# One-token gated attention and MLP on one core: the sixth value tile loaded in one transfer, the seventh in three, and the output projection's Pool-queue rows moved as 32 KB pieces instead of 16 KB

## The chip, the cores and the metric

The kernel runs on one core of a Trainium2 chip, in one launch. The metric is the device time in microseconds (us). The kernel before took 192.69 us, the median of three runs (192.54 to 192.71).

## The reference

One token of 512 numbers goes through two branches, which a gate mixes. Everything is bfloat16.

```python
g = sigmoid((x * gate_w).sum(-1))
q = (x @ wq) as 32 heads of 128
scores = q . k_cache * 128**-0.5        # 32 heads, 4096 cached keys each
p = softmax(scores)
a = (p @ v_cache, heads joined) @ wo    # wo is 4096 x 512
h = relu(x @ w1 + b1) ** 2              # 1376 wide
b = h @ w2 + b2
out = g * a + (1 - g) * b
```

The two caches are 32 MB each, `wq` and `wo` 4 MB each, `w1` and `w2` 1.4 MB each. Every byte is read once.

## The kernel before

**Tiles.** Four heads make a group, so there are NT = 8 groups and 8 key tiles and 8 value tiles. A tile is 128 partitions of 32 KB, 4 MB: each head has 32 partitions, each with B = 128 consecutive keys of 128 numbers. All tiles, and late in the kernel the tile "m" of small weights, go through five buffers of the tensor `ring`, in the order of the list `LOADS`: k0, k1, k2, v0, k3, v1, k4, v2, k5, v3, k6, v4, k7, v5, v6, m, v7. The SP queue issues them in that order. Before each, the function `free` (L304 to L310) waits until the buffer's last user is done: for a key tile VectorE's products and TensorE's transposes, for a value tile TensorE's products with it.

**Compute.** A group is worked in U = 4 units. Of a key tile's 128 columns VectorE multiplies 80 with the query (`ttr`, L734; 96 in the last tile), and TensorE transposes the other 48, which ScalarE copies out and TensorE multiplies with the query (`transposes`, `evac`, `scores`). Maximum, exponentials and the products with the value tile (`pv`) follow. TensorE's program is a loop over i from 0 to NU + 1 with NU = 32 units; the table `PV` says which `pv` units are run at which i. For the last groups the table is written by hand: units 20 and 21 (the first half of v5, the sixth value tile) at i = 30, units 22 to 27 (the rest of v5 and all of v6) at i = 32, after the last scores. The four units of v7 come later, behind the output projection's first part.

**Values in parts.** `PARTS` names the value tiles that are loaded in several transfers, and where they are cut, in columns. Each part has a semaphore of its own, and `pv` waits for a part at the unit that starts on its cut. Before, v5 comes in two parts of 64 columns, v6 in four of 32, v7 in parts of 40, 40, 36 and 12. A row of 64 columns is 16 KB in one partition, one of 32 columns 8 KB. A tile that is not in `PARTS` comes in one transfer of 32 KB rows, and `landed` waits for its buffer's semaphore.

**wo.** The projection's weights for 28 of the 32 heads are 112 rows of 32 KB, and each row goes to one partition of the tensor `W`, where `wq` was before. They follow when the queries are made (`started`). The list `FIRST` has eight transfers of three rows each, which SP issues between v0 and k3 (L325). The list `RUNS` has ten transfers, which the Pool queue issues (L376): rows 24, 24, 4, 8, 4, 8, 4, 8, 2 and 2, 88 in all. A run has a number e and a width k. `place` puts its rows on partitions from 32 + 4e + r on, or from 4e + r on (64 + 4e + r from e = 8), four partitions further for each step of e. `turns` reckons a position `at` from 0 to 15 that a run of width k moves on by k; where the next run's e is not the present position, a dummy transfer of d rows is issued ahead of it to make up the difference (L373). Seven such dummies are issued, of 4, 4, 4, 4, 4, 3 and 2 rows; each row is two pieces of 8 bytes. The runs' e are 4, 4, 4, 8, 4, 8, 4, 8, 3 and 7, their widths k 12, 12, 4, 8, 4, 8, 4, 8, 2 and 2. `max_dma_last_dim=16384` cuts each 32 KB row of a run into two pieces; the transfers of `FIRST` have no such cap. Which row landed in which partition is undone at the end by the 0/1 matrix `selA` (`spread_a`).

**End.** After VectorE's last products: the sums and outputs of groups 5 and 6, `spread_a`, 22 of the 32 column blocks of `wo` on TensorE (`out_a`) and 10 on VectorE (`rows_v`), the MLP, the four units of v7, then `out_b` with the last four heads' rows of `wo` (the last transfers but one), `mlp_out`, and the store.

Of the kernel before, what the change touches and what calls it, by code (L numbers as in the profile page):

```python
# [5 lines left out]
def bass_gated_mix__gqa_block_cached__dense_activation_squared_relu__decode_kernel(  # L6
# [34 lines left out]
    NT = NH // R  # L41
    B = 4096 // P

    U = 4
    NU = NT * U
# [7 lines left out]
    PV = {i: [i - LAG] for i in range(LAG, LAG + (NT - 3) * U)}  # L53
# [2 lines left out]
    PV[27] = [18, 19]  # L56
    for i in (28, 29, 30):
        del PV[i]
    PV[NU - 2] = [NU - 3 * U, NU - 3 * U + 1]
    PV[NU] = list(range(NU - 3 * U + 2, NU - U))  # L60

    PARTS = {NT - 3: [0, 64, B], NT - 2: [0, 32, 64, 96, B], NT - 1: [0, 40, 80, 116, B]}

    GR = [(0, 8), (8, 16), (16, 24), (24, 28), (28, 32)]
    NG = len(GR)
# [32 lines left out]
    def turns():  # L98
        at, out = 0, []
        for _, e, k, _, _ in RUNS:  # L100
            d = (e - at) % 16
            out.append((False, d) if d != 1 else (True, e))
            at = (e + k) % 16
        return out
# [29 lines left out]
    with ctx:  # L134
# [6 lines left out]
        def sem(name):  # L141
            return ctx.enter_context(nc.semaphore(name))
# [3 lines left out]
        def held(kind, j=0):  # L146
            return ring[:, AT[kind, j] % SLOTS, :]
# [93 lines left out]
        s_wp = [sem(f"s_wp{n}") for n in range(len(RUNS))]  # L241
        s_dm = [sem(f"s_dm{n}") for n in range(len(RUNS))]
        s_wr = sem("s_wr")
        s_wk = sem("s_wk")
        s_vl = {(j, n): sem(f"s_vl{j}{n}") for j in PARTS for n in range(len(PARTS[j]) - 1)}
        s_sel = sem("s_sel")
# [65 lines left out]
        def started(eng):  # L312
            eng.wait_ge(s_qps, NT)
            eng.wait_ge(s_g, 4)
            eng.wait_ge(s_b1c, 1)

        @block.sync
        def _(eng):
            for n, (kind, j) in enumerate(LOADS):  # L320
                free(eng, n)
                if n == SLOTS - 1:
                    started(eng)
                    for p, st, k, q in STRIPS[len(RUNS):]:
                        eng.dma_start(W[p:p + st * (k - 1) + 1:st, :], woa_v[q:q + k, :]).then_inc(s_wr, 16)  # L325
                if kind == "v" and j in PARTS:
                    for w in range(len(PARTS[j]) - 1):
                        part = slice(PARTS[j][w] * 128, PARTS[j][w + 1] * 128)
                        eng.dma_start(held("v", j)[:, part], v_v[j][:, part]).then_inc(s_vl[j, w], 16)  # L329
                elif kind in "kv":  # L330
                    eng.dma_start(held(kind, j), (k_v if kind == "k" else v_v)[j])\
                       .then_inc(s_l[n % SLOTS], 16)
                elif kind == "m":
                    eng.dma_start(held("m")[:, 0:W2], w1_v).then_inc(s_w[0], 16)
                    eng.dma_start(held("m")[:, W2:W3], w2_v).then_inc(s_w[1], 16)
            for c in range(len(TS) - 1):
                eng.dma_start(wob_sb[:, TS[c]:TS[c + 1], :], wob_v[:, TS[c]:TS[c + 1], :])\
                   .then_inc(s_wo[c], 16)
            eng.dma_start(w2b, B_w2[F - 128:F, :]).then_inc(s_w[2], 16)
            eng.wait_ge(s_f4, 1)  # L340
            eng.dma_start(out[0, 0, :].rearrange("(j p) -> j p", p=128), fin4).then_inc(s_out, 16)

        @block.gpsimd
        def _(eng):
            eng.memset(ident[:, :], 0.0).then_inc(s_id, 1)
            eng.memset(identf[:, :], 0.0).then_inc(s_id, 1)
            eng.memset(onesf[:, :], 1.0).then_inc(s_cst, 1)
            eng.wait_ge(s_id, 2)
            for m in (ident, identf):  # L350
                eng.affine_select(out=m[:, :], in_=m[:, :], compare_op=ALU.not_equal, fill=1.0,
                                  base=0, pattern=[[-1, 128]], channel_multiplier=1)\
                   .then_inc(s_id, 1)
            eng.memset(RS[:, :], 0.0).then_inc(s_cst, 1)
            eng.memset(E[:, :, :, :], 0.0).then_inc(s_cst, 1)
            eng.memset(selA[:, :, :], 0.0).then_inc(s_sel, 1)
            eng.wait_ge(s_sel, 1)
            for n, (p, st, k, q) in enumerate(STRIPS):
                eng.wait_ge(s_sel, n + 1)
                part = selA[:, :, p:p + st * (k - 1) + 1]  # L360
                eng.affine_select(out=part, in_=part, compare_op=ALU.not_equal, fill=1.0, base=-st * q,
                                  pattern=[[st, 4], [-1, st * (k - 1) + 1]], channel_multiplier=4 * st)\
                   .then_inc(s_sel, 1)

            started(eng)
            sent = 0
            for n, ((back, d), run) in enumerate(zip(turns(), RUNS)):
                if back:
                    eng.inc_swdge_sem([], [], mode="reset_dge_cursor")  # L370
                if d:
                    src = B_w1[0:d, 0:32].rearrange("p (a c) -> p a c", a=2)
                    eng.dma_start(dm[0:d, sent, :, 0:4], src[:, :, 0:4]).then_inc(s_dm[sent], 16)  # L373
                    sent += 1
                p, st, k, q = STRIPS[n]
                eng.dma_start(W[p:p + st * (k - 1) + 1:st, :], woa_v[q:q + k, :],  # L376
                              max_dma_last_dim=16384).then_inc(s_wp[n], 16)
            for n in range(sent):
                eng.wait_ge(s_dm[n], 16)
            eng.wait_ge(s_wr, 16 * len(FIRST))  # L380
            for q in s_wp[:-1]:
                eng.wait_ge(q, 16)
            eng.wait_ge(s_wp[-1], 16)
            eng.memset(tick[:, :], 0.0).then_inc(s_wk, 1)
# [76 lines left out]
        def _(eng):  # L461
# [82 lines left out]
            def pv(u):  # L544
                j, w = u // U, u % U
                lo, hi = w * B // U, (w + 1) * B // U
                if j == NT - 1:
                    lo, hi = PARTS[j][w:w + 2]
                if j in PARTS:
                    if lo in PARTS[j]:  # L550
# [320 lines left out]
```

## Time and profile before

| | before |
|---|---|
| median of three runs | 192.69 us |
| the profiled execution | 192.5 us, of which the span from first to last instruction 191.1 us |
| VectorE, TensorE, ScalarE busy | 83%, 64%, 44% of the span |
| moved by DMA | 78.70 MB, mean 412 GB/s |
| packets | 5298, of them 768 on the Pool queue (q0), 2.89 MB |
| mean granted TensorE clock | 0.674 |

The span is cut into 40 slices in the page's second part; a digit there is the busy share in tenths. SPq and POOLq are the queues that issue transfers; a "landing" is the time from the issue of a transfer to its semaphore. The trace also has a record of every DMA packet, with its queue, size, start and duration, but without the engine that moved it.

### The profile page before, as it was taken

The numbers are of one execution on the slowest core, as the hardware profiler recorded it, in microseconds if no ns is written. First come the engines' busy times: TensorE is split into PE (matmuls) and PEld (weight loads), VectorE is DVE, ScalarE is ACT, GpSimd is POOL, SyncE is SP. The second block draws the span as 40 slices with busy tenths as digits, with TensorE's granted clock in tenths as the row PEclk, the third lists the DMA queues.
The fourth block names the chain that finished last, engine by engine and source line by source line (L and its number), as shares of the span: only waits on it lengthen the run. The fifth ranks groups of instructions, "written<-read, shape, count | busy, mean of one in ns | idle before, by whom it ended". The sixth has DMA issues, their size and how long they took to land.

```text
span 191.1 us, 5609 instructions
## 1 busy us (share of the span) xinstructions
PE 122.1 (64%) x1864; PEld 92.8 (49%) x1866; DVE 158.6 (83%) x1387; ACT 84.3 (44%) x207; POOL 18.4 (10%) x48
## 2 busy tenths in 40 slices
PE   0019764644524694898499986845876488548975
PEld 0014343534413543276256544745876277437964
DVE  0031399999999999999999999998999799998821
ACT  2013975825843654077409542943644293000400
POOL 7630000990000000000000000000000000000000
PEclk9999998555555558699859759955555555555555
DMA  6999999999999999999999999999999999999992
GB/s 219 440 440 439 439 439 430 439 398 451 432 424 405 432 406 432 442 420 439 442 427 422 425 434 425 417 424 432 425 430 435 398 424 406 419 421 426 414 388 72
DMA packets 5298, 78.70 MB, mean 412 GB/s; under 512 B 1099, under 2 KB 1741, under 8 KB 1870
## 3 DMA queue, kind: packets, MB, share of 16 engines
q1 hardware_dynamic: 4488, 75.47, 93.1%
q0 software_dynamic: 768, 2.89, 3.7%
q8 instruction: 14, 0.23, 0.5%
q14 instruction: 14, 0.11, 0.2%
q10 hardware_dynamic: 14, 0.01, 0.0%
HBM read 78.35 MB, written 0.00 MB: 410 GB/s over the span
## 4 chain that ended last, share of the span: by engine, by line
DVE 46%; DMA 38%; SPq 7%; PE 4%; ACT 2%; issue 2%; DVEq 0%; ACTq 0%
DVE ring L734 43%; DMA ring<-in_A_k_cache_dram 25%; DMA ring<-in_A_wo_dram 14%; SPq L329 6%; DVE S L734 2%; PE pX L562 2%; ACT E L434 1%; PE KP L516 1%; PE pO L576 1%; ACT kT L415 0%; DVE gm L748 0%; DVE gx L751 0%; ACT parts L440 0%; PE pQ L637 0%; DVE mp L741 0%
## 5 line engine op out<-in xcount | busy, mean ns | idle before, releaser
L734 DVE CUSTOM_DVE_ANT_0 ring<-ring,qb 128x128 bf16<-128x128 bf16 x656 | 140.6, 281 | 1.4 <-DMA ring<-in_A_k_cache_dram 1.3
L415 ACT ACTIVATE kT<-KP 128x768 bf16<-128x768 bf16 (+1 forms) x64 | 46.6, 779 | 47.1 <-PE pQ L529 19.0
L734 DVE DVE_READ_ACCUMULATOR2_ANT S<- 128x1 f32 x656 | 50.5, 77 | 0.1
L516 PE MATMUL KP<-ident,ring 128*128 128x128 bf16 x368 | 37.9, 275 | 9.5 <-DMA ring<-in_A_k_cache_dram 6.2
L516 PEld LDWEIGHTS KP<-ident,ring 128*128 128x128 bf16 x368 | 30.9, 126 | 14.1 <-DMA ring<-in_A_k_cache_dram 6.5
L562 PE MATMUL pX<-ring,E 128*16 128x512 bf16 x72 | 24.0, 493 | 0.0
L434 ACT ACTIVATE E<-S,nM 32x128 bf16<-32x128 f32 x32 | 18.6, 580 | 1.0
L570 PE MATMUL pO<-E,ring 128*128 128x4 bf16 x352 | 10.8, 166 | 4.9 <-DMA ring<-in_A_v_cache_dram 4.9
L570 PEld LDWEIGHTS pO<-E,ring 128*128 128x128 bf16 x352 | 10.2, 102 | 5.3 <-DMA ring<-in_A_v_cache_dram 5.2
L536 PE MATMUL pM<-identf,mp 128*1 128x128 f32 x8 | 3.0, 370 | 15.1 <-DVE mp L741 15.1
L562 PEld LDWEIGHTS pX<-ring,E 128*16 128x16 bf16 x72 | 6.9, 106 | 11.5 <-issue 7.7
L570 PE MATMUL pX<-E,ring 128*128 128x4 bf16 x384 | 11.3, 166 | 1.6 <-DMA ring<-in_A_v_cache_dram 1.6
L570 PEld LDWEIGHTS pX<-E,ring 128*128 128x128 bf16 x384 | 11.0, 105 | 1.8 <-DMA ring<-in_A_v_cache_dram 1.8
L426 ACT ACTIVATE nM<-pM 128x1 f32<-128x1 f32 x8 | 1.4, 174 | 19.0 <-PE pM L541 19.0
L529 PE MATMUL pQ<-qcol,kT 128*128 128x4 bf16 x176 | 7.7, 168 | 2.3 <-ACT kT L415 2.3
L541 PE MATMUL pM<-onesf,gx 1*128 1x1 f32 x16 | 4.2, 329 | 7.0 <-DVE gx L751 7.0
L529 PEld LDWEIGHTS pQ<-qcol,kT 128*128 128x128 bf16 x176 | 7.1, 105 | 3.1 <-ACT kT L415 3.1
L536 PEld LDWEIGHTS pM<-identf,mp 128*1 128x1 f32 x8 | 0.7, 85 | 16.3 <-DVE mp L741 16.1
L700 DVE CUSTOM_DVE_ANT_0 ring<-ring 1x512 bf16<-1x512 bf16 x1 | 0.7, 680 | 9.4 <-DMA ring<-in_gate_w_dram 9.4
L529 PEld LDWEIGHTS pS<-qcol,kT 128*128 128x128 bf16 x192 | 7.4, 106 | 1.7 <-issue 1.7
L434 ACT ACTIVATION_READ_ACCUMULATOR E<-S,nM 32x1 f32 x32 | 8.1, 253 | 0.0
L529 PE MATMUL pS<-qcol,kT 128*128 128x4 bf16 x192 | 7.7, 168 | 0.0
(88 smaller groups left out, 109.0 us busy)
## 6 DMA issues: line engine op xcount, KB each, us to landing
ring<-in_A_k_cache_dram SPq DMA_DIRECT2D x8, 4096.0 KB, 29.5
ring<-in_A_v_cache_dram SPq DMA_DIRECT2D x5, 4096.0 KB, 29.0
W<-in_A_wq_dram SPq DMA_DIRECT2D x1, 4096.0 KB, 12.4
ring<-in_A_v_cache_dram SPq DMA_DIRECT2D x2, 2048.0 KB, 27.7
ring<-in_A_v_cache_dram SPq DMA_DIRECT2D x4, 1024.0 KB, 27.7
ring<-in_A_v_cache_dram SPq DMA_DIRECT2D x2, 1280.0 KB, 31.9
W<-in_A_wo_dram POOLq DMA_DIRECT2D x2, 768.0 KB, 17.9
ring<-in_B_w_dram SPq DMA_DIRECT2D x1, 1376.0 KB, 25.3
```

The costliest lines, as they stand in the source:

```text
L329: eng.dma_start(held("v", j)[:, part], v_v[j][:, part]).then_inc(s_vl[j, w], 16)
L415: eng.activation(kT[:, n % NC, 0:HB[u // U] * 128], KP[n % 3][:, 0:HB[u // U] * 128], ACT.Copy).then_inc(s_ev, 1)
L426: eng.activation(nM[:, j:j + 1], MB[:, j:j + 1], ACT.Copy).then_inc(s_nm, 1)
L434: eng.activation(E[rows, j % NE, :, r], S[rows, j % NS, :], ACT.Exp, bias=nM[rows, j:j + 1], scale=SCALE, accum_out=RS[rows, R * j + r:R * ...
L516: mm = eng.transpose(KP[n % 3][:, y * 128:(y + 1) * 128], held("k", j)[:, b * 128:(b + 1) * 128], ident[:, :])
L529: mm = eng.matmul(S2[j % 2][:, c:c + R], kT[:, n % NC, y * 128:(y + 1) * 128], qcol[:, R * j:R * j + R], start=True, stop=True)
L536: eng.transpose(MT[0:1, :], mp[:, j:j + 1], identf[:, :]).then_inc(s_mt, 1)
L541: eng.matmul(MB[:, j:j + 1], gx[0:1, j % 2, :], onesf[0:1, 0:1], start=True, stop=True).then_inc(s_mb, 1)
L562: mm = eng.matmul(pX[0:4 * R, :], E[:, j % NE, b:b + 4, :].rearrange("p b r -> p (b r)"), held("v", j)[:, b * 128:(b + 4) * 128], start=(b ...
L570: mm = eng.matmul(O(R * j, R * j + R), held("v", j)[:, b * 128:(b + 1) * 128], E[:, j % NE, b, :], start=(b == n * B // U), stop=(n == 0 a ...
L576: mm = eng.matmul(O(R * j, R * j + R), parts[:, b * 128:(b + 1) * 128], identf[0:4 * R, R * b:R * b + R], start=False, stop=(b == 3), skip ...
L734: ins = eng.tensor_tensor_reduce(kb, kb, qb[:, j, :], 1.0, 0.0, ALU.mult, ALU.add, S[:, j % NS, b:b + 1])
```

## The change

The sixth value tile, v5, is no longer in `PARTS` and comes in one transfer. v6 comes in three parts, of 64, 32 and 32 columns. Units 20 and 21 of `pv` go from i = 30 to i = 32, ahead of units 22 to 27. The ten transfers of `RUNS` have a cap of 32768 bytes for a piece, so that a row of 32 KB is one piece. The dummies and their rows, `place`, `turns` and `FIRST` are as before.

```diff
-    PV[NU - 2] = [NU - 3 * U, NU - 3 * U + 1]
-    PV[NU] = list(range(NU - 3 * U + 2, NU - U))
-
-    PARTS = {NT - 3: [0, 64, B], NT - 2: [0, 32, 64, 96, B], NT - 1: [0, 40, 80, 116, B]}
+    PV[NU] = list(range(NU - 3 * U, NU - U))
+
+    PARTS = {NT - 2: [0, 64, 96, B], NT - 1: [0, 40, 80, 116, B]}
...
                 eng.dma_start(W[p:p + st * (k - 1) + 1:st, :], woa_v[q:q + k, :],
-                              max_dma_last_dim=16384).then_inc(s_wp[n], 16)
+                              max_dma_last_dim=32768).then_inc(s_wp[n], 16)
```

## The prediction

> **What bounds the kernel.** I read the page's slices and queues first, then the chain of waits, then TensorE's timeline at the end, then the records of the DMA packets.
>
> ```profile
> DMA  6999999999999999999999999999999999999992
> GB/s 219 440 440 439 439 439 430 439 398 451 432 424 405 432 406 432 442 420 439 442 427 422 425 434 425 417 424 432 425 430 435 398 424 406 419 421 426 414 388 72
> q1 hardware_dynamic: 4488, 75.47, 93.1%
> q0 software_dynamic: 768, 2.89, 3.7%
> ```
>
> The 16 DMA engines are full from the second slice to the last but one. By the packet records they never run dry between 5 us and 186 us. The Pool queue's share, 3.7%, is wo's ten runs.
>
> ```profile
> 161.90 26.23 DMA ring<-in_A_wo_dram
> 188.27 0.56 PE pQ L637 x16
> 188.84 0.28 PE pQ L628 x4
> 189.37 0.28 PE KP L690
> 189.67 0.21 DVE ring L839
> ```
>
> The chain ends with a transfer that was issued at 161.90 and landed at 188.13: it stood 26 us in a full queue, so a faster or slower issue is nothing to it. Behind it 3.0 us of tail. The time of this execution is 192.5 = 188.1 + 3.0 + 1.4 outside the span; the median is 192.69, 0.2 above.
>
> ```profile
> 160.68 1.87 PE L570 MATMUL pX<-E,ring 128*128 128x4 bf16 x64
> 163.17 1.01 PE L570 MATMUL pO<-E,ring 128*128 128x4 bf16 x32 [0.19 <-DMA ring<-in_A_v_cache_dram]
> 165.64 1.01 PE L570 MATMUL pO<-E,ring 128*128 128x4 bf16 x32 [1.46 <-DMA ring<-in_A_v_cache_dram]
> 168.22 1.01 PE L570 MATMUL pO<-E,ring 128*128 128x4 bf16 x32 [1.57 <-DMA ring<-in_A_v_cache_dram]
> 170.88 1.02 PE L570 MATMUL pO<-E,ring 128*128 128x4 bf16 x32 [1.64 <-DMA ring<-in_A_v_cache_dram]
> 186.27 1.44 PE L570 MATMUL pX<-E,ring 128*128 128x4 bf16 x48 [0.65 <-DMA ring<-in_A_v_cache_dram]
> ```
>
> TensorE waits for data at each quarter of v6 and again, 0.65 us, before the end of v7. VectorE is 83% busy but waits for k6 and k7 too, 0.61 and 0.65 us (131.29 and 150.84 in its timeline). All follow the stream.
>
> A stream ends with its slowest engine, so what each engine has to move counts. The trace names no engine, but the times at which shares of a transfer end show them. After the eight transfers of `FIRST` (24 rows of 32 KB, three a transfer) three shares of k3 end at 71.2 to 71.7, the others mostly at 66.8 to 68.6: three engines carry eight rows each. At k6 fifteen shares end within 127.7 to 129.7, one at 130.8. So the Pool rows went to the others and evened the load; that is what `turns` and the dummies are for. The widths show too: the first 16 KB pieces come in a burst of 12 (40.07 to 40.54), later ones in bursts of 4 (59.5, 61.3) and 8 (64.7).
>
> **Part by part.**
>
> *v5 whole, v6 in three.* Median packet: 1.214 us for 32 KB, 0.614 for 16 KB, 0.312 for 8 KB. Per engine v5 is 8 x 1.214 = 9.71 in place of 16 x 0.614 = 9.82; v6's first half 8 x 0.614 = 4.91 in place of 16 x 0.312 = 4.99. Saved: 0.19 us. SP issues two transfers fewer, about 0.4 us each, hidden by the 26 us of queue.
>
> *`pv` of units 20 and 21 later.* On TensorE they are moved past the scores of unit 30, the transposes of unit 31 and its scores: 64 matmuls, 1.85 us at 156.51. After the change 128 matmuls begin at 160.5 and end at 164.2, the sum at L585 (0.57) at 164.8. v6's first half lands, as its second quarter now, at 165.6; then 64 matmuls, 1.9 us, until 167.5, and the next quarter at 168.2. Cover 0.7 us at both places, so I price this at nothing; without the cover it would add at most what the 0.65 us before 186.27 doesn't take. Nobody else waits: VectorE asks for unit 23 only at 171.33, no buffer and no exponential waits for units 20 to 23, and the scores of units 30 and 31 come up to 1.85 us earlier, to no use.
>
> *wo's rows in one piece.* By packets alone: 2 x 0.611 becomes about 1.214 a row, nothing. Pool issues the same 17 transfers (0.55 to 0.62 us each), and its wait for them, over at 99.76, is needed only at 172.
>
> What isn't shown is where whole rows go. The dummies could do with one piece a row, yet are written with two, as the runs were; `FIRST`, on SP's queue, has whole rows. No row of the trace has whole rows on Pool's queue. Two bounds: (a) the steering holds, no change; (b) each run starts at the first engine, whatever stands before it. In (b) a 24-row run puts two rows on each of engines 0 to 11, the others one row on each of the first 4, 8 or 2. Engines 0 and 1 then get 2 + 2 + 3 x 1 + 3 x 1 + 2 x 1 = 12 rows that they don't have now, beside the 8 of `FIRST`: 20, where now the fullest have 8. I take (b): the two pieces stand in the code exactly at the transfers that are steered and nowhere else, and the cap that made them is what is changed.
>
> [...]
>
> Price of (b): 12 x 1.214 = 14.6 us on engine 0, if a row costs what it costs now. The three `FIRST` engines are not the last at present: two have their share of k7 at about 148.9 and 149.1, the last engine at 150.4, and data stop between 186.1 and 188.4. So 1.5 us are swallowed. About 20 packets in the trace take some 0.6 us more than their kind, 1.25 an engine; those two engines show none, so I add 0.7. Net 14.6 - 1.5 + 0.7 - 0.2 = 13.6, for 206.1.
>
> Upwards: `place` gives each row the partitions of the engine that was to bring it. Under (b) the rows of engine 0 go to partitions that other engines are writing just then. Nothing in the trace prices that; two writers that take turns at worst double the packet, 12 x 1.214 = 14.6 more. The four rows from the wide runs are nearest to now, since all twelve writers are shifted alike and stay out of each other's way: price 0. For the other eight I take the middle between single and double, 8 x 0.61 = 4.9. Sum: 192.5 + 13.6 + 4.9 = 211.0.
>
> [...]
>
> What is late next under (b): k3 to k7 land later by what engine 0 has taken on, and VectorE, which has only 1.3 us of such waits now, waits some 13 to 18 us in all; its tail shifts with k6 and k7, and the end stays with the stream.
>
> **Rivals.**
>
> 1. *The steering holds* (not slower). For it: nothing in `turns`, `place` or the order is changed, and SP's whole rows keep to three engines. Against it: the two-piece dummies. It decides if k6's shares still end within about 3 us. The gains then stand alone, 0.2 of stream (0.06 more where an engine has eight Pool rows): 192.4. Chance 14%.
> 2. *Whole rows spread over 16 engines, but from the cursor.* Only dummies move the cursor then. Adding up the ten runs, engines 0 to 2 get 5 rows beside their 8: 5 x 1.214 = 6.1, less 1.5, plus 0.7, less 0.2, and up to half as much again for shared partitions: about 199. For it: a cursor is what the dummies turn. Against it: a spread over all needs no start. Chance 6%.
> 3. *`pv` late.* If v5's one landing came after 161.2, units 20 to 23 would end behind v6's first half and the delay go on through the sums at L764 to `rows_v`, at most 1 us over the 0.65 of slack: 193.0. Against it: v5's rows are ahead of v6's in the queue, and its second half does not delay 160.68 now. Chance 2%, counted with slower.
>
> Forecast, (b): 78%.
>
> **Numbers.** (b) gives 206.1 with undisturbed rows and 215.9 with eight doubled; 211.0 is its middle. The range goes down to rival 2 and leaves out rival 1 and the far end of doubling: 199 to 216. Runs of this kernel differ by 0.17 us, so about 0.2% (0.39 us) can be told from no change; rival 1's gain of 0.1% mostly can't. Faster 6%, same 8% (both from rival 1), slower 86%.
>
> **What would show it.** Right: 88 packets of 32 KB on q0; shares of k6 that end more than 10 us apart, two last; VectorE waiting for key tiles by over 10 us; a mean of 370 to 385 GB/s (78.70 MB over some 209 us), 9s in the DMA row giving way to 8s and 7s; a landing of the key tiles longer than 29.5 us; the same 3 us tail. Packets on q0 longer than 1.3 us would show shared partitions, 1.21 us would bring 206. Wrong: the row of 9s and 412 GB/s unchanged. Then the end is at 188, and only 0.2 us have gone.

## The result and the profile after

The changed kernel takes 226.26 us, the median of six runs (225.51 to 226.74), beside 192.61 for the kernel before: a ratio of 1.174 (95% interval 1.173 to 1.176), 33.7 us slower. The forecast had the direction and the place, but 211.0 us and at most 216. The profiled execution took 226.74, its span 225.4. Executions over 1.5% above the fastest of their kernel, one of `cursor0` and one of `crossed`, are left out of the times and ratios below.

The page of the changed kernel, slices and queues (one slice is now 5.6 us):

```profile
DMA  7999999998999999899968999999999999999320
GB/s 279 437 402 465 425 406 465 282 353 215 345 279 291 260 262 250 244 361 361 413 269 334 465 385 445 449 390 458 385 451 445 394 420 428 416 409 364 129 107 30
q1 hardware_dynamic: 4200, 75.47, 86.2%
q0 software_dynamic: 576, 2.89, 5.4%
```

Two losses can be seen. From the eighth slice to the nineteenth the engines are as busy as before by the packet records, but move 215 to 361 GB/s, not some 430: the packets themselves are slow. And at the end, 129, 107 and 30 GB/s: four engines are far behind and work alone. The trace's semaphore records show when each share of a transfer ends: of the transfer at the end of the chain below, twelve end between 206.8 and 209.5 us, the other four singly at 220.2, 221.0, 221.7 and 222.4. Between these two losses, in slices 20 to 22, engines stand idle (52 us, summed over the 16 engines).

VectorE's and SP's waits of the changed kernel (engine, line, waited for: us in total, times, longest), and VectorE's timeline where the longest one ends:

```profile
DVE ring L733 <- DMA ring<-in_A_k_cache_dram: 34.0, 5, 30.0
SPq L330 <- PE pO L575: 67.4, 3, 42.3
106.54 0.29 DVE L733 CUSTOM_DVE_ANT_0 ring<-ring,qb 128x128 bf16<-128x128 bf16 x1 [29.99 <-DMA ring<-in_A_k_cache_dram]
```

VectorE waits 34.0 us for key tiles, where it waited 1.3. Thirty of them are one wait, for k3, the tile that follows `FIRST` and shares its time with all of wo's runs. Twelve of its shares end by 85.5 us, the last three at 105.7 to 106.5. While it is missing no buffer comes free, so SP can't issue (42.3 us), and that is the idle of slices 20 to 22. After k3 the kernel runs as it did, late: k6 begins at 165.43 (131.29 before), the span ends 34.3 us later.

The end of the chain of waits has the old form, with a tail of 3 us:

```profile
191.52 30.86 DMA ring<-in_A_wo_dram
222.53 0.56 PE pQ L636 x16
```

The packet records give the sizes. wo's runs are now 88 packets of 32 KB, with a median of 2.18 us each. A row cost two pieces of 0.611 before. Of the tiles' 32 KB packets 348 took over 1.5 us, before 35. Summed over wo's pieces and the 32 KB packets of SP's queue, the time above 1.213 us (0.611 for 16 KB) was 28.4 us before and is 372.2 now: 343.8 more, or 21.5 us for each of 16 engines. I call this the extra packet time.

### The profile page after: what moved, and what is told of

Read it like the earlier page. It is cut to its first block, busy times and chain, and to the rows that moved or that the text cites. A ratio compares the mean times of both kernels' runs of the same rounds, so it can differ in the third digit from the quotient of the medians.

```text
span 225.4 us, 5609 instructions
## 1 busy us (share of the span) xinstructions
PE 122.1 (54%) x1866; PEld 93.1 (41%) x1866; DVE 158.9 (70%) x1387; ACT 84.1 (37%) x207; POOL 18.1 (8%) x48
## 4 chain that ended last, share of the span: by engine, by line
DMA 31%; DVE 26%; another core or an unknown queue 16%; PE 14%; ACT 5%; SPq 4%; issue 3%; ACTq 0%; POOL 0%; POOLq 0%; DVEq 0%
DVE ring L733 24%; DMA ring<-in_A_wo_dram 14%; DMA ring<-in_A_k_cache_dram 13%; PE pX L561 5%; DMA ring<-in_B_b_dram 5%; SPq L328 3%; PE KP L515 3%; ACT E L433 2%; PE pQ L493 2%; ACT kT L414 1%; DVE S L733 1%; ACT qb L405 1%; PE pO L575 1%; PE pX L493 1%
## 5 line engine op out<-in xcount | busy, mean ns | idle before, releaser
L561 PE MATMUL pX<-ring,E 128*16 128x512 bf16 x72 | 23.2, 480 | 2.9 <-DMA ring<-in_A_v_cache_dram 2.9
L799 DVE SCALAR_TENSOR_TENSOR ring<-W,o2f,ring 128x512 f32<-128x512 bf16 x9 | 6.8, 751 | 0.3
## 6 DMA issues: line engine op xcount, KB each, us to landing
ring<-in_A_k_cache_dram SPq DMA_DIRECT2D x8, 4096.0 KB, 30.3
ring<-in_A_v_cache_dram SPq DMA_DIRECT2D x2, 1024.0 KB, 30.3
```

The costliest lines, as they stand in the source:

```text
L561: mm = eng.matmul(pX[0:4 * R, :], E[:, j % NE, b:b + 4, :].rearrange("p b r -> p (b r)"), held("v", j)[:, b * 128:(b + 4) * 128], start=(b ...
L799: eng.scalar_tensor_tensor(out=vsum[:, :], in0=wo_sb[:, TP + t, :], scalar=o2f[:, t:t + 1], in1=vsum[:, :], op0=ALU.mult, op1=ALU.add).the ...
```

## The experiments

Each experiment is the kernel before with the edit shown, unless said otherwise. Where a row has an interval, it is that of the ratio to the kernel before on the same chip.

**1. The two halves of the change.** `parts_only` is the changed kernel with the old cap, `cap_only` the kernel before with the new one.

```diff
 # cap_only; parts_only has all the other lines of the change
-                              max_dma_last_dim=16384).then_inc(s_wp[n], 16)
+                              max_dma_last_dim=32768).then_inc(s_wp[n], 16)
```

> The value tiles' cuts and the order of pv as in the changed kernel, wo's runs in two pieces of 16 KB as before. All theories: the 33.7 us come from the runs, so 192.4 (0.2 under before, from 0.19 us of stream), tiles' packets at 1.21 us throughout. Rival: the tiles' cuts or the late pv have a share in the loss, 193 or more.

> Before with wo's runs in one piece of 32 KB, nothing else changed. All theories: the whole loss, 225.5 to 227. Rival: if the tiles' cuts take part, several us less than 226.

Measured: `parts_only` 192.60 beside 192.72, ratio 0.9993 (0.9984 to 1.0002); `cap_only` 225.1, ratio 1.169 (1.166 to 1.173). The loss is the cap's: 32.4 of the 33.7 us. The tiles' cuts alone gain 0.1 us, which the measurement can't tell from nothing (by the interval, 0.3 gained to nothing). `cap_only` lies 0.4 under what was expected and 1.2 under the changed kernel. Its extra packet time is 326 us, 1.1 less than the changed kernel's for each of 16 engines; whether the tiles' cuts add that under the new cap isn't shown. TensorE's timeline of `parts_only` shows the late `pv`:

```profile
161.11 3.57 PE L569 MATMUL pX<-E,ring 128*128 128x4 bf16 x128 [1.22 <-DMA ring<-in_A_v_cache_dram]
166.01 1.87 PE L569 MATMUL pO<-E,ring 128*128 128x4 bf16 x64 [0.90 <-DMA ring<-in_A_v_cache_dram]
168.48 1.02 PE L569 MATMUL pO<-E,ring 128*128 128x4 bf16 x32 [0.60 <-DMA ring<-in_A_v_cache_dram]
170.97 1.01 PE L569 MATMUL pO<-E,ring 128*128 128x4 bf16 x32 [1.47 <-DMA ring<-in_A_v_cache_dram]
186.37 1.44 PE L569 MATMUL pX<-E,ring 128*128 128x4 bf16 x48 [0.54 <-DMA ring<-in_A_v_cache_dram]
```

TensorE waits for v5's single landing and starts 0.6 us after the 160.5 that was forecast, but still waits 0.90, 0.60 and 1.47 us for v6's three parts and 0.54 before the end: the work stays covered.

**2. Where whole rows go.** `cursor0` keeps two pieces a row and the dummies, and sets the Pool queue's cursor back just ahead of each run.

```diff
                 p, st, k, q = STRIPS[n]
+                eng.inc_swdge_sem([], [], mode="reset_dge_cursor")
                 eng.dma_start(W[p:p + st * (k - 1) + 1:st, :], woa_v[q:q + k, :],
```

> Before with two pieces a row, but the Pool queue's engine cursor set back to the first engine just ahead of every run, so that two-piece runs start where the forecast put whole rows. Theory A (whole rows start at the first engine, and rows written to another engine's partitions are slow on both sides): pieces of 16 KB at 0.95 to 1.2 us, tiles' packets at 1.5 us or more meanwhile, 218 to 228 us. Theory B (whole rows from the Pool queue are slow in themselves, beside the uneven load): pieces stay at 0.61 us and only the uneven load is left, 12 rows on two engines, 204 to 208 us. Theory C (whole rows stay steered and are slow in themselves): also 204 to 208, and the changed kernel would not share its pattern.

Measured: 225.58, ratio 1.169 (1.167 to 1.172), the same ratio as `cap_only`. Pieces of 16 KB now take 0.895 us (median), with 42 of 176 between 0.65 and 0.8, so Theory A's lower bound for a piece was a little high; its time holds. Size and form of the pieces are not the cause; the engine at which a run starts is.

`matched` and `whole_at4` look at it from the other side: whole rows, laid for the engines that get them if a run starts at the first. In `matched` these are four runs of 16 rows. In `whole_at4` they are four runs of 8 rows, each behind a dummy that leaves the cursor at the fifth engine; the other half of those rows comes in two pieces.

```diff
 # matched
-    RUNS = [(INNER, 4, 12, 0, 2), (INNER, 4, 12, 1, 2),
+    RUNS = [(INNER, 0, 16, 0, 1), (INNER, 0, 16, 1, 1), (INNER, 0, 16, 2, 1), (INNER, 0, 16, 3, 1),
             (OUTER, 4, 4, 0, 1), (OUTER, 8, 8, 0, 1), (OUTER, 4, 4, 1, 1), (OUTER, 8, 8, 1, 1),
-            (OUTER, 4, 4, 2, 1), (OUTER, 8, 8, 2, 1),
-            (OUTER, 3, 2, 3, 1), (SEAM, 7, 2, 3, 1)]
-    FIRST = ...
+            (OUTER, 4, 4, 2, 1), (OUTER, 8, 8, 2, 1), (OUTER, 8, 3, 3, 1)]
+    FIRST = [(OUTER, 0, 3, 0, 1), (OUTER, 0, 3, 1, 1), (OUTER, 0, 3, 2, 1)]
...
-                              max_dma_last_dim=16384).then_inc(s_wp[n], 16)
+                              max_dma_last_dim=32768 if k == 16 else 16384).then_inc(s_wp[n], 16)
 # whole_at4, against matched: cursor to 4 ahead of each whole run, to 8 ahead of the others
+    RUNS = [*[(INNER, e, 8, r, 1) for r in range(4) for e in (0, 8)],
...
+            if kind == INNER:
+                out.append((True, 4 if e == 0 else 8))
...
+                              max_dma_last_dim=32768 if run[:2] == (INNER, 0) else 16384).then_inc(s_wp[n], 16)
```

> 64 of the rows as four runs of 16 whole rows of 32 KB on the Pool queue, laid so that the i-th row is on the i-th engine's partitions if a run of whole rows starts at the first engine; the other 48 rows in two pieces, steered, or on SP. Engine 3 gets three rows more than before, the others 7 or 8. Theory A: whole rows at 1.21 us and no tile packet slowed, 192.5 to 196. Theory B (whole rows from the Pool queue are slow in themselves): whole rows at 2.0 us or more, tiles' packets slowed beside them, over 205.

> As matched (same rows on every engine), but the whole rows are four runs of 8, laid for the first eight engines, and ahead of each a dummy leaves the cursor at the fifth engine. If whole rows start at the first engine whatever the cursor is: whole rows at 1.21 us, nothing slowed, 195 to 197 as matched. If they start at the cursor: all 32 of them are on another engine's partitions, whole rows at 2 us, tiles' packets slowed, 203 or more.

Measured: `matched` 195.99, ratio 1.017 (1.015 to 1.019); `whole_at4` 196.43, ratio 1.019 (1.017 to 1.021). In both the whole rows take 1.213 us (median), and the tiles' packets stay at 1.213 to 1.218. So whole rows are not slow in themselves, and with the cursor at the fifth engine they still start at the first. The 3.2 and 3.8 us over before agree with three more rows on engine 3, 3 x 1.213 = 3.6: in both, one share of a late transfer ends 2.6 to 2.9 us behind all others.

**3. The price of other engines' partitions, with even load.** `crossed` was meant for it and wasn't what it was meant to be.

```diff
 # crossed
-    RUNS = [(INNER, 4, 12, 0, 2), (INNER, 4, 12, 1, 2),
+    RUNS = [(INNER, 4, 8, 0, 2), (INNER, 12, 4, 0, 2), (INNER, 4, 8, 1, 2), (INNER, 12, 4, 1, 2),
...
-        for _, e, k, _, _ in RUNS:
+        for kind, e, k, _, _ in RUNS:
+            if kind == INNER:
+                e = 8 if e == 4 else 4
```

> Before with two pieces a row and every engine as many rows as before, but the two 24-row runs cut in 16 and 8 rows whose engines are exchanged, so that 48 of 88 rows are written by an engine four or eight places from the one whose partitions they are. Theory A: the 96 pieces of these rows take over 0.9 us and the other 80 pieces 0.61; four rows an engine by 0.6 to 1.2 us more each, and tiles' packets beside them slower, 195 to 202 us. Theories B and C: all pieces 0.61 us, 192.4 to 193.

Measured: 219.94, ratio 1.142 (1.137 to 1.147), well over what was expected, with slow pieces to the end (in the profiled execution, of 224.3 us, median 0.99 us). The bursts of the kernel before were 12 wide for 24 rows, 8 for 8 and 4 for 4; how wide a run of 16 rows in two pieces goes is in no view. If it is not the eight that `turns` reckons with, the cursor is wrong for every later run, nearly all rows are misplaced, and the load can be uneven too. So it settles nothing by itself. `split_home` and `split_crossed` mend it with runs of 8 and 4 rows:

```diff
 # split_home
-    RUNS = [(INNER, 4, 12, 0, 2), (INNER, 4, 12, 1, 2),
+    RUNS = [*[(INNER, e, k, r, 1) for r in range(4) for e, k in ((4, 8), (12, 4))],
 # split_crossed: split_home, and
+            if kind == INNER:
+                e = 8 if e == 4 else 4
```

> Control for split_crossed: before, with the two 24-row runs cut into eight runs of 8 and 4 rows on the same engines and partitions. Pieces 0.61 us; more turns on the Pool queue, hidden; 192.4 to 193.5.

> The same sixteen runs, but the 8-row runs go to the engines of the 4-row runs and their next ones, and the other way round: every engine has as many rows as in split_home, 48 of 88 rows are written to another engine's partitions. [...] Theory A (another engine's partitions): 96 pieces of 0.75 to 1.3 us, tiles' packets beside them at 1.4 us or more, 200 to 212 us. Theory D (what was lost in the last runs is uneven load alone): pieces 0.61 us, 192.4 to 193.5.

Measured: `split_home` 192.79, ratio 1.0005 (0.9995 to 1.0014); `split_crossed` 206.80, ratio 1.072 (1.067 to 1.077). 48 rows written by an engine that is not their partitions' own cost 14.0 us with the load as even as before. An engine's own partitions are those that `place` pairs with its position in `turns`; no view names them, and what shows the pairing is these two kernels, with the same transfers and the pairing kept (192.79) or broken (206.80). Page of `split_crossed`:

```profile
DMA  7999999999999999999999999999999999999991
GB/s 251 457 425 413 411 451 459 392 336 310 360 339 344 342 315 299 305 355 418 447 413 443 418 426 434 427 421 427 430 435 418 408 419 410 422 418 428 414 354 39
```

The eighth to the eighteenth slice, about 36 to 92 us, are slow with full engines; then the crossed runs are through and 408 to 447 come back. While they last pieces take 0.80 to 0.86 us and the tiles' packets 1.52 to 1.72 (medians of 10 us, 40 to 90 us); afterwards 0.61 and 1.22. And the last slices are as before: no engine is left behind.

`sp_crossed` asks whether it is the Pool queue's affair: twelve of `FIRST`'s whole rows, issued by SP, change places with twelve Pool rows.

```diff
 # sp_crossed, against split_home
-    RUNS = [*[(INNER, e, k, r, 1) for r in range(4) for e, k in ((4, 8), (12, 4))],
+    RUNS = [*[(INNER, e, k, r, 1) for r in range(4) for e, k in ((4, 9), (0, 3))],
-    FIRST = [(INNER, 0, 3, 0, 1), (INNER, 0, 3, 1, 1), (INNER, 0, 3, 2, 1), (INNER, 0, 3, 3, 1),
+    FIRST = [(INNER, 13, 3, 0, 1), (INNER, 13, 3, 1, 1), (INNER, 13, 3, 2, 1), (INNER, 13, 3, 3, 1),
...
+            if kind == INNER and k == 3:
+                e = 13
```

> As split_home, but twelve of FIRST's 24 rows, which SP issues as whole rows on the first three engines, go to the partitions of engines 13 to 15, and twelve Pool rows of engines 13 to 15 to the partitions of the first three. The load stays even. Theory A, and whichever queue the rows come from: slow packets on both queues, 24 of 112 rows crossed, by split_crossed's 14.0 us for 48 rows some 4 to 9 us, 197 to 202. Theory A': only the Pool queue's crossed rows matter, 24 pieces, 194 to 197, SP's whole rows at 1.21. If crossing matters only where many engines do it at once: under 193.5.

Measured: 201.12, ratio 1.044 (1.040 to 1.047), 8.5 us for 24 rows. The tiles' packets are slow in four stretches. In three of them, 40 to 48, 68 to 74 and 80 to 87 us, only three Pool rows are out of place, and each stretch has some 19 us of extra packet time; in the fourth, 52 to 63 us, three Pool rows and the twelve of `FIRST` are, and it has 64. So either queue's rows do it (64 beside 19 us), and six engines, by `place`, are enough.

`halves` does without wo: the second value tile comes as two transfers of 64 partitions.

```diff
+                elif kind == "v" and j == 1:
+                    eng.dma_start(held("v", j)[0:64], v_v[j][0:64]).then_inc(s_ex, 16)
+                    eng.dma_start(held("v", j)[64:128], v_v[j][64:128]).then_inc(s_l[n % SLOTS], 16)
```

> Before, with the second value tile loaded in two transfers of 64 partitions instead of one of 128: each transfer still runs on 16 engines, four rows each, but two engines at a time write to the partitions that one of them has in a full tile. It prices two engines that share partitions in step, on SP's queue alone. If they take turns: eight packets an engine of 2.4 us instead of 1.2, 9.7 us on the stream, 201 to 203. If sharing costs more than turns: packets of 3 us or more, 206 or over. If sharing costs only where the Pool queue is in it: 192.6 to 193.5.

Measured: 214.28, ratio 1.112 (1.110 to 1.114): 21.6 us for one tile, over twice what taking turns would cost (9.7 by estimate, 8 x 1.213). By `place` partitions 0 to 63 are those of eight engines, 64 to 127 those of the other eight. Page of `halves`:

```profile
DMA  7999999999999999999999999999999999999970
GB/s 290 401 419 468 394 479 400 411 456 404 445 419 308 186 166 219 203 189 213 379 450 408 444 434 402 456 422 416 447 419 417 425 416 405 423 420 419 419 292 12
```

Six slices at 166 to 219 GB/s with the DMA row at 9, so with all 16 engines at work, and one of 308 ahead of them: 37 us, for what would hold up the stream for 9.7 if the engines took turns. Tiles' packets that start in 70 to 80 us take 3.19 us (median), wo's pieces beside them 1.47, though these go where they belong.

By these rates the six slices moved some 6.3 MB (an estimate, 1176 GB/s x 5.32 us), more than the tile's 4.19: other data moved in the slow stretch too.

**4. The price of uneven load alone.** `load01` and `load01b` copy 24 more rows from wo to a spare place in device memory, two a transfer.

```diff
+    spare = nc.dram_tensor("spare", [24, 33 * DM], bf16).ap()      # load01: 32 * DM
...
+                    for x in range(12):
+                        eng.dma_start(spare[2 * x:2 * x + 2, 0:32 * DM], woa_v[2 * x:2 * x + 2, :]).then_inc(s_ex, 16)
```

> Before, and beside it twelve transfers of two rows of 32 KB from wo to a spare place in device memory on SP's queue, between FIRST and k3: twelve rows more on each of the first two engines, none of them written to the on-chip memory. It prices the uneven load of the changed kernel without the other engines' partitions. If a row costs 1.21 us: 192.6 + 14.6 - 1.5 = 205 to 207. If uneven load in itself makes the tiles' packets slow: 215 or more.

Measured: 195.63, ratio 1.015 (1.013 to 1.016). The rows lie one behind the other at both ends here, and came as 192 packets of 4 KB, sixteen for each transfer; no engine is left behind. It prices only 0.8 MB more, 24 x 1.213 / 16 = 1.8 us, of 2.9 measured; the rest is not explained.

> As load01, but the rows of the spare place in device memory are 33 KB apart, so that the copy isn't merged and dealt over all engines as load01's 4 KB packets show it was: twelve rows more on each of the first two engines, nothing written to the on-chip memory. If uneven load costs what the rows cost: 192.7 + 14.6 - 1.5 = 204 to 207, tiles' packets 1.21 us. If uneven load in itself slows the tiles' packets or starves the stream: 215 or more.

Measured: 206.36, ratio 1.072 (1.070 to 1.074): 13.8 us, inside the expected range. Page of `load01b`:

```profile
DMA  7999999999999999999899999999999999998110
GB/s 263 449 417 410 429 476 420 429 396 445 439 408 432 415 445 429 436 423 405 336 429 424 426 431 436 423 429 432 416 416 421 412 423 418 422 419 315 71 55 19
```

The stream runs at its normal rate but for slice 20, packets at 1.21 us, and two engines finish alone at 71 and 55 GB/s. That is an end like the changed kernel's without its slow middle, as `split_crossed` is the slow middle without this end. In the changed kernel four engines finish alone, at 129 and 107 GB/s: by bound (b) the whole rows also put ten more on each of the third and the fourth engine (2 + 2 + 3 + 3). The two fullest have twelve more, as here.

**The sum.** For kernels with even load, extra packet time spread over 16 engines, beside what was measured:

| | extra packet time / 16 | measured loss | loss of the profiled execution |
|---|---|---|---|
| `sp_crossed` | 7.9 us | 8.5 us | 8.7 us |
| `split_crossed` | 11.6 us | 14.0 us | 12.6 us |
| `halves` | 19.0 us | 21.6 us | 21.5 us |
| changed kernel | 21.5 us, and 13.8 from `load01b` | 33.7 us | 34.1 us |

The last row adds up to 35.3, 1.6 too many. Counted in the changed kernel's profiled execution itself, all packets took 339 us more than before, 21.2 for each engine, and the time without a packet grew by 13.0 for each: 3.3 of it in slices 20 to 22, nearly all the rest in the last four. Together they are the 34.3 by which its span is longer. Why the second part is 13.0, with four engines behind, and not 13.8 isn't shown.

## Why the prediction was wrong

- *What bounds the kernel, and the end that follows the stream.* Right: the tail is 3 us still, and all the loss is in the stream.
- *v5 whole, v6 in three, `pv` late.* Right: 0.19 us forecast, 0.1 measured and not to be told from nothing; rival 3 did not come.
- *Whole rows start at the first engine.* Right, and now shown: `cursor0` gives nearly the changed kernel's time with the old pieces (225.58 beside 226.26), and in `whole_at4` whole rows take 1.213 us on the first engines' partitions with the cursor at the fifth. Rows in two pieces follow the cursor (`split_home`, 0.611 us a piece, 192.79). Rivals 1 and 2 fall.
- *Twelve rows more on two engines, 13.6 net.* Right in the price: 13.8 in `load01b`. That it comes so near is luck in part: the 0.7 us for slow packets rests on about 20 of them, but the trace before has 35 of 32 KB alone over 1.5 us, and 28.4 us of extra packet time, 1.8 for each engine. And it counted only the two fullest engines; four are behind at the end.
- *"Upwards": the rows on other engines' partitions, 4.9.* This is the step that failed. The term measures about 20 (33.7 - 13.8; 21.5 by the extra packet time). It was mis-sized in three ways. Only the rows of engine 0 were counted, eight of them, but all 88 crossed, and packets of other engines were slow with them, which came back as late tiles: the tiles' packets took 264 of the 344 us of extra packet time. The wide runs' rows were priced at nothing because twelve writers shifted alike should stay out of each other's way; the first twelve whole rows, which start at 40.0 to 40.5, took 1.74 to 2.35 us. And double was taken as the worst, on the author's estimate that two writers take turns, which no run shows; in `halves` the tiles' packets took 3.19 us, 2.6 times 1.213, so the far end of 215.9 was no bound.
- *What would show it.* 88 packets of 32 KB, longer than 1.3 us, and key tiles later than 29.5 us (30.3) came true. The mean rate was put at 370 to 385 GB/s and is 349; VectorE's waits at 13 to 18 us and are 34.0. Shares of k6 end 15.3 us apart, more than 10 as forecast, but four are last, not two: twelve end by 151.8 us, four from 163.2 to 165.4. The DMA row keeps its 9s, but for a few slices, until it breaks off at the end.

**Still open:** why sharing costs more than taking turns, and how far a slow packet spreads to engines that share nothing with it. The runs show that it does, not by what path: in `sp_crossed` six engines bring or own the misplaced rows, but of 80 tile packets that start between 52 and 63 us 69 take over 1.5 us, and six engines can move at most 6 x 11 / 1.5 = 44 such packets in that time. Open too is the 1.2 us between `cap_only` and the changed kernel.

## What to carry to other kernels

In a kernel that is bound by its DMA stream, ask of each edit to a transfer's shape which engine will move each row and which engine writes those partitions otherwise; in `cursor0` bytes, pieces and transfers stayed the same while the time moved by 17% (192.72 to 225.58 us). Price a misplaced row by what it does to all engines' packets, not by its own engine's: here 48 misplaced rows of 32 KB cost 14.0 us, 0.29 us a row, with the load even. And read the rate row beside the busy row: here engines at 9 with half the GB/s had slow packets (`halves`, 166 to 219 GB/s, 3.19 us), and slices at 1 to 3 at the end came with uneven load (`load01b`, 71 and 55 GB/s; changed kernel, 129 and 107).

## What the runs showed of the hardware that was not expected

- One 4 MB tile in two transfers of 64 partitions, by `place` two engines in step on the partitions of one, cost 21.6 us (`halves`); taking turns would have cost 9.7 by estimate (8 x 1.213).
- A run of 8 whole rows on the Pool queue took 1.213 us a row on the partitions paired with the first eight engines, with the cursor at the fifth (`whole_at4`), while two-piece runs follow the cursor (`split_home`, 0.611 us a piece; 0.895 with the cursor set back, `cursor0`).
- Whole rows of 32 KB from the Pool queue cost what they cost from SP's, 1.213 us (median), where the partitions are the engine's own (`matched`).
